# Gates of two heads on two halves of the rows, one chain for all other gates, and one copy for queries and keys of a pair, in a forgetting attention with a SwiGLU block

## The chip, the core and the metric

The kernel runs on one core of one Trainium2 chip. The metric is the device time of one execution in microseconds (us); several executions give a median. A hardware profile of one execution shows every instruction with its engine and its time. The engines are PE (matrix multiplication), PEld (its weight loads), DVE (VectorE), ACT (ScalarE), POOL (GpSimd) and SP (SyncE, which here only issues DMA transfers). POOL and ACT issue DMA transfers as well.

## The reference

q, k and v have 8 batches, 8 heads, 576 positions and 64 dimensions; f has 8 x 8 x 576. The attention adds a decay to the scores and feeds a gated block of 4608 tokens (8 x 576), 512 features and 1536 hidden features:

```python
scores = scale * np.matmul(q, k.transpose(0, 1, 3, 2))
log_f = np.log(np.clip(f, 0.0001, 1.0))
cum = np.cumsum(log_f, axis=-1)
decay = cum[:, :, :, None] - cum[:, :, None, :]
scores = np.where(causal, -1000000000.0, scores + decay)
attn = softmax(scores)            # with the maximum taken off first
x = matmul(attn, v), heads joined # 4608 x 512
g = x @ w_gate
out = (g * sigmoid(g) * (x @ w_val)) @ w_out
```

The values of `cum` are called gates here. A score needs `cum` of its query added and `cum` of its key taken off. In bfloat16 one number is too coarse for a key's gate, so it is kept as a sum of three (high, middle, low).

## The kernel before, in words

A small planner in the kernel (class `Plan`) decides the order of the instructions on each engine when the program is built. Each operation has an engine, an estimated duration, a key (lower goes first), a time `ready` before which it is not started, and what it waits for. On the chip each engine then runs its list strictly in that order and waits at semaphores. Constants such as `PACE0` (when batch 2's queries may be fetched) and `W_KEY` are inputs of this planner.

**Batch 0** is handled apart (`four`, `attention2`, `score2`). POOL loads q and k of eight heads by DMA, PE transposes them (L482), ACT and DVE copy them from PSUM into `QK` (L303 and L305 are the lines of the common copy helper: L303 on ACT, L305 on DVE or POOL). Head jj lies on rows 0 to 63 and head jj+4 on rows 64 to 127. A score group covers one of four parts of the key and query blocks for such a pair of heads (`BANKS`: 384, 512, 384 and 320 columns per head for the parts 0 to 3, so 1600 in all and 1216 in the parts 1 to 3). L641 multiplies queries and keys, 64 rows for each head. The gates are added by further matmuls into the same PSUM bank, over all 128 rows: `KG` holds the keys' gates of 32 heads in four row groups (a group of ones, high, middle, low), and the query side picks one head's rows. For the parts 1 to 3 this is L650, with a copy of the query side masked for that head (`choose`, L374). For the first part (the heads in `ONEHOT`, all of them) it is two matmuls without such a copy, L652 and L653.

**Gates.** `gates` loads f of batches 0 to 3 four times onto 128 rows, then clip (L324, DVE), ln (L327, ACT), a scan in two parts (L331, DVE) and the split into high, middle and low (L342 to L352). `dec_out` (L358) writes the rows for 32 heads to a DRAM buffer. The gates of batches 4 to 7 (32 heads on 32 rows, `lf1`) are loaded at the start and scanned and split later (`later`, L331, L362 to L370; `DEC1_AT = 36`), and four further `dec_out` write them.

**Batch 1** (`quad`): POOL loads q and k into natural order, PE transposes 128 columns at a time (`turn`, L498) with two pairs of heads one above the other in PSUM, and each half is copied to rows 0 to 63 of its pair's slot of `QK` (`straighten`, 16 copies of 64 rows). `rows` (L522) loads four gate rows for queries and keys from DRAM into rows 64 to 67 of that slot, so that one matmul of 68 rows (L623) gives score and decay together. Batches 2 to 7 get their transposed q and k through DRAM by DMA transposes on SP (`narrow`, `turned`) and their gate rows by `rows` as well.

**Then** ACT takes the exponential (L658), POOL masks the diagonal blocks (L667), PE multiplies with v (L681, 65 columns: 64 and one of ones for the sum), DVE takes the reciprocal and scales (L688, L693), and the result is transposed (L698 and a copy, or a DMA transpose on SP). The gated block is L826 (both first products), L830 (tanh on ACT), L834 and L837 (DVE), L841 (last product) and L845. The first 512 tokens go in two pieces of 256, woven into batch 1's attention. Idle PE is filled early by dummy matmuls (L930).

## Time and profile before

| what | us |
|---|---|
| median of 3 runs (lowest, highest) | 389.0 (388.3, 389.59) |
| the profiled execution's own time | 388.2 |
| span of its profile | 386.5 |
| first score of batch 0 (L641) | 10.43 |
| first score of batch 1 (L623) | 33.25 |
| first L841 | 67.75 |
| first score of batch 2 | 84.02 |
| last PE start | 382.85 |

The span runs from the first to the last instruction of the program in the profile. A busy share is an average over stages with different limits, so the stages are read one at a time: the table gives their borders. Where a line shows a group of instructions, the time from the start of one group to the start of the next says what the group costs in a stream; the duration of one matmul contains its way through the array and is longer. A wait is put down to what came last.

### The profile page before, as it was taken

How to read it: one execution, taken by the hardware profiler on the slowest of the kernel's cores; microseconds unless marked ns; L12 is line 12 of the kernel's file. 1: busy time of each engine (PE TensorE's matmuls, PEld its weight loads, DVE VectorE, ACT ScalarE, POOL GpSimd, SP SyncE). 2: the span in 40 equal slices, each digit the busy share in tenths (PEclk: the TensorE clock that was granted, in tenths of full speed). 3: DMA queues.
4: the chain of work that ended last, by engine and by line, in shares of the span. 5: the costliest groups of instructions: out<-in, count | busy, mean ns of one | idle time of the engine just before them, and what ended most of it. 6: DMA issues, size and time to landing. Idle time of an engine off the chain costs nothing.

```text
span 386.5 us, 8511 instructions
## 1 busy us (share of the span) xinstructions
PE 375.8 (97%) x3185; PEld 216.1 (56%) x3185; DVE 219.5 (57%) x460; ACT 213.8 (55%) x440; POOL 140.1 (36%) x368
## 2 busy tenths in 40 slices
PE   6997999999999999999999999999999999999996
PEld 4666789545556555555555555555564444444444
DVE  8957988257624773277515772477427725733750
ACT  5978884246756565755666457566673323323322
POOL 8794658005534624444355236522330000000000
PEclk9999999999999999999999999999999999999999
DMA  8999998769679994999699999995131011002003
GB/s 165 194 193 195 206 194 133 170 168 171 124 171 204 154 194 94 210 223 180 128 182 199 197 138 213 231 151 85 46 90 46 0 54 57 0 28 83 0 2 109
DMA packets 125065, 52.01 MB, mean 135 GB/s; under 512 B 111840, under 2 KB 119392, under 8 KB 124256
## 3 DMA queue, kind: packets, MB, share of 16 engines
q1 hardware_dynamic: 108640, 36.18, 46.9%
q0 software_dynamic: 16288, 15.14, 26.9%
q8 instruction: 25, 0.41, 0.4%
q10 hardware_dynamic: 96, 0.15, 0.1%
q14 instruction: 16, 0.13, 0.1%
HBM read 38.63 MB, written 17.11 MB: 144 GB/s over the span
## 4 chain that ended last, share of the span: by engine, by line
PE 94%; DVE 2%; ACT 2%; issue 1%; POOL 0%; DVEq 0%; POOLq 0%
PE ps L826 47%; PE ps L841 24%; PE ps L623 9%; PE ps L681 7%; PE ps L650 2%; ACT QK L303 1%; PE ps L641 1%; PE ps L930 1%; PE ps L698 1%; DVE QK L305 1%; PE ps L652 0%; DVE hh L837 0%; PE ps L482 0%; PE ps L498 0%; PE ps L653 0%
## 5 line engine op out<-in xcount | busy, mean ns | idle before, releaser
L826 PE MATMUL ps<-xT,wg 128*128 128x512 bf16 (+1 forms) x480 | 113.0, 357 | 1.1 <-DVE QK L305 1.0
L830 ACT ACTIVATE th<-ps 128x512 f32<-128x512 f32 (+1 forms) x120 | 66.5, 554 | 86.0 <-PE ps L826 83.6
L826 PE MATMUL ps<-xT,wv 128*128 128x512 bf16 (+1 forms) x480 | 113.0, 357 | 0.5 <-DMA wg<-in_moe_w_gate_dram 0.5
L834 DVE SCALAR_TENSOR_TENSOR th<-th,ps 128x512 f32<-128x512 f32 (+1 forms) x120 | 75.6, 630 | 64.9 <-ACT th L830 64.6
L658 ACT ACTIVATE PT<-ps 128x512 bf16<-128x512 f32 (+2 forms) x192 | 92.6, 508 | 27.6 <-PE ps L623 15.8
L841 PE MATMUL ps<-wo,hh 128*128 128x512 bf16 (+2 forms) x456 | 104.5, 367 | 0.0
L837 DVE TENSOR_TENSOR hh<-th,ps 128x512 bf16<-128x512 f32 (+1 forms) x120 | 76.0, 634 | 13.6 <-PE ps L826 1.8
L667 POOL TENSOR_SCALAR_AFFINE_SELECT PT<-PT 128x128 bf16<-128x128 bf16 (+1 forms) x192 | 52.9, 282 | 71.9 <-ACT PT L658 67.2
L826 PEld LDWEIGHTS <-wg 128*128 128x128 bf16 x480 | 45.5, 97 | 41.2 <-issue 1.4
L826 PEld LDWEIGHTS <-wv 128*128 128x128 bf16 x480 | 45.4, 97 | 37.5 <-issue 0.4
L623 PE MATMUL ps<-QK 68*128 68x256 bf16 x392 | 64.8, 261 | 0.0
L841 PEld LDWEIGHTS <-hh 128*128 128x128 bf16 x456 | 41.8, 97 | 37.1
L667 POOL TENSOR_SCALAR_AFFINE_SELECT PTa<-PTa 128x256 bf16<-128x256 bf16 x64 | 26.2, 412 | 76.1 <-ACT PTa L658 74.9
L688 DVE RECIPROCAL rc<-ps 128x5 f32<-128x5 f32 (+2 forms) x68 | 12.9, 190 | 65.5 <-PE ps L681 65.1
L681 PE MATMUL ps<-VB,PT 128*128 128x65 bf16 x768 | 44.2, 193 | 0.8 <-ACT QK L303 0.8
L681 PEld LDWEIGHTS <-PT 128*128 128x128 bf16 x768 | 37.0, 97 | 13.0 <-issue 1.0
L845 ACT ACTIVATE ot<-ps 128x512 f32<-128x512 f32 (+2 forms) x38 | 21.9, 575 | 39.9 <-PE ps L841 38.2
L623 PEld LDWEIGHTS <-QK 68*128 68x128 bf16 x392 | 31.1, 97 | 13.7
L658 ACT ACTIVATE PTa<-ps 128x384 bf16<-128x384 f32 x64 | 30.9, 488 | 10.3 <-PE ps L623 9.5
L693 DVE TENSOR_TENSOR xn<-ps,rc 128x320 bf16<-128x320 f32 (+2 forms) x72 | 32.3, 453 | 2.2
L681 PEld LDWEIGHTS <-PTa 128*128 128x128 bf16 x192 | 13.7, 98 | 11.3
L305 POOL CAST VB<-natv 128x512 bf16<-128x512 f32 (+1 forms) x32 | 19.0, 613 | 0.2 <-DMA natv<-in_v_dram 0.2
(69 smaller groups left out, 158.6 us busy)
## 6 DMA issues: line engine op xcount, KB each, us to landing
out_dram<-ot SPq DMA_DIRECT2D x35, 256.0 KB
natv<-in_v_dram SPq DMA_DIRECT2D x25, 256.0 KB
qk_d<-in_q_dram POOLq DMA_DIRECT2D x24, 144.0 KB, 3.6
qk_d<-in_k_dram POOLq DMA_DIRECT2D x24, 144.0 KB, 4.3
wg<-in_moe_w_gate_dram POOLq DMA_DIRECT2D x3, 512.0 KB, 11.1
wv<-in_moe_w_val_dram POOLq DMA_DIRECT2D x3, 512.0 KB, 12.4
wo<-in_moe_w_out_dram POOLq DMA_DIRECT2D x4, 384.0 KB, 11.9
xT<-in_q_dram POOLq DMA_DIRECT2D x4, 288.0 KB, 8.7
```

The lines of the kernel that those rows point to most:

```text
L305: E[e].tensor_copy(dst, src)
L623: nc.tensor.matmul(s[:, c : c + w], QK[:KR, hqk[p].i, 1, j * S + kt * P : j * S + (kt + 1) * P], QK[:KR, hqk[p].i, 0, j * S + q0 : j * S + ...
L658: nc.scalar.activation(place(h, i)[:, OFFS[i] : OFFS[i] + c], ps(bs)[:, :c], AF.Exp, scale=0.125)
L667: nc.gpsimd.affine_select(out=d, in_=d, pattern=pat, compare_op=ALU.is_ge, fill=0.0, base=0, channel_multiplier=-1,)
L681: nc.tensor.matmul(o[:, lo : lo + D + 1], pt[:, c : c + P], VB[hvb[b].i][:, kt, hb, : D + 1], start=first and n == 0, stop=last and n == l ...
L693: nc.vector.tensor_mul(XN[bx.i][:, qb : qb + nq, j], o, r)
L826: nc.tensor.matmul(ps(bf)[:, :n], w[:, ko, fc * P : (fc + 1) * P], xT[:, ko, t0 : t0 + n], start=(ko == 0), stop=(ko == KD - 1))
L830: nc.scalar.activation(TH[bt.i][:, :n], ps(bf)[:, :n], AF.Tanh, scale=0.5)
L834: nc.vector.scalar_tensor_tensor(out=t, in0=t, scalar=1.0, in1=ps(bf)[:, :n], op0=ALU.add, op1=ALU.mult)
L837: nc.vector.tensor_mul(HH[bh.i][:, lo : lo + n], TH[bt.i][:, :n], ps(bf)[:, :n])
L841: nc.tensor.matmul(ps(bf)[:m, c], HH[hs[fc].i][:, lo : lo + m], wo[:, fc, c], start=(fc == 0), stop=(fc == KF - 1))
L845: nc.scalar.activation(OT[bo.i][:m, c], ps(bf)[:m, c], AF.Copy, scale=0.5)
```

## The change

Four things are changed together.

1. **Batch 0's gates on halves of the rows.** f of batch 0 alone is loaded, eight times: rows 0 to 31 hold four copies of its 8 heads, rows 64 to 95 four more; the other rows are set to 1. In each half the 8-row groups of `KG` become ones, high, middle and low, by multiplying with constants per row (`ct`). A query side `QG[jj]` serves both heads of a pair, one on each half. So the gate matmuls have 64 rows for each head, as the score matmuls have. There are four masked copies for parts 1 to 3 instead of eight.
2. **All other gates in one chain.** `lf1` holds all 64 heads on 64 rows; the later chain makes all rows that go to DRAM, planned from 12 us on (`DEC1_AT`), and only its four `dec_out` are left. Its clip runs on POOL. The `rows` of batch 1 now wait for these.
3. **One copy for queries and keys of a pair.** `turn` puts q on rows 0 to 63 and k on rows 64 to 127 of PSUM for one pair; `straighten` copies 128 rows at once (8 copies in all). `lower`, a new DMA on SP, moves the keys to rows 0 to 63 of the pair's other half slot; `rows` of that pair follows it, since it writes over rows 64 to 67.
4. **Constants.** `PACE0` from 61 to 57; all five tiles of batch 1's v are cast by POOL's DMA (`V_CAST`), where two went through `natv`; smaller DMA durations in the planner, and the order of the transposes (`S1_KEY`, `U1`).

```diff
-    def ld_f(e, half, n):
-        E[e].dma_start(out=lf1 if half else lf[GR * n : GR * (n + 1)],
-                       in_=f.rearrange("b h s -> (b h) s")[GR * half : GR * (half + 1)])
+    def ld_f(e, n):
+        if n == 8:
+            E[e].dma_start(out=lf1, in_=f.rearrange("b h s -> (b h) s"))
+        else:
+            u, t = divmod(n, 4)
+            E[e].dma_start(out=lf[D * u + H * t : D * u + H * (t + 1)], in_=f[0])
...
+    def hi(e, c):
+        nc.vector.tensor_scalar_mul(KG[:, c], cum[:, c], -8.0)
+    def less(e, n, c):
+        nc.vector.scalar_tensor_tensor(out=r1[:, c], in0=KG[:, c], scalar=ct[:, 4 + n : 5 + n], in1=r1[:, c] if n else cum[:, c],
+                                       op0=ALU.mult, op1=ALU.add)
+    def mid(e, c):
+        nc.vector.tensor_scalar_mul(KG[:, c], r1[:, c], -8.0)
+    def low(e, c):
+        nc.vector.tensor_scalar(out=KG[:, c], in0=r1[:, c], scalar1=ct[:, 6:7], scalar2=ct[:, 3:4], op0=ALU.mult, op1=ALU.add)
...
+    def choose(e, jj, c):
+        s1, s2 = ct[:, 12 + jj : 13 + jj], ct[:, 8 + jj : 9 + jj]
         if e == "ACT":
+            nc.scalar.activation(QG[jj][:, c], cum[:, c], AF.Identity, scale=s1, bias=s2)
         else:
+            nc.vector.tensor_scalar(out=QG[jj][:, c], in0=cum[:, c], scalar1=s1, scalar2=s2, op0=ALU.mult, op1=ALU.add)
+    def dec_out(e, n):
+        nc.sync.dma_start(out=dec_dram[0, 0] if n == 0 else dec_dram[n, 1], in_=late[n])
...
-        out1 = [op(("SP", SPi), dec_out, 1, n, after=l, key=DEC1_KEY, dma=0.15, packet=50, tag="decout") for n in range(4)]
+        need = [l[:1], l[1:2], l[3:4], l[4:]]
+        out1 = [op(("SP", SPi), dec_out, n, after=need[n], key=-7, dma=0.3, packet=50, tag="decout") for n in range(4)]
...
-    def turn(e, b, g, x, n, bt):
+    def turn(e, g, u, n, bt):
         t0, nt = PH[n]
         t = ps(bt).bitcast(BF16)
         for i in range(nt):
-            for u in range(2):
-                nc.tensor.transpose(t[D * u : D * (u + 1), i * P : (i + 1) * P],
-                                    QN[b][2 * g + x][:, u, (t0 + i) * D : (t0 + i + 1) * D], ident)
+            for x in range(2):
+                nc.tensor.transpose(t[D * x : D * (x + 1), i * P : (i + 1) * P],
+                                    QN[1][2 * g + x][:, u, (t0 + i) * D : (t0 + i + 1) * D], ident)
...
+    def straighten(e, p, n, bt):
         t0, nt = PH[n]
+        dst = QK[:, hqk[p].i, 0, : 2 * S].rearrange("p (j c t) -> p j c t", j=2, t=QT)[:, :, :, t0 : t0 + nt]
+        copy(e, dst, ps(bt).bitcast(BF16)[:, : nt * P].rearrange("p (t j c) -> p j c t", t=nt, j=2))
+    def lower(e, p):
+        nc.sync.dma_start(out=QK[:D, hqk[p].i, 1, : 2 * S], in_=QK[D:, hqk[p].i, 0, : 2 * S])
...
+            done.append(op(("SP", SPi), lower, p, after=done, use=[hqk[p]], key=key, dma=0.5, packet=93, tag=("lower", p)))
+            r = op(("SP", SPi), rows, p, after=done + out1 + o_out1, use=[hqk[p]], key=key, dma=0.25, packet=60, tag=("rows", p))
...
         for n, (kt, q0, w, c) in enumerate(segs):
             for u in range(2):
-                s, h, end = ps(bs[u]), jj + 4 * u, n == len(segs) - 1
-                m = min(P, S - kt * P)
-                keys = KG[:, kt * P : kt * P + m]
+                r, m, end = slice(D * u, D * (u + 1)), min(P, S - kt * P), n == len(segs) - 1
+                o, keys = ps(bs[u])[:m, c : c + w], KG[r, kt * P : kt * P + m]
                 if i or jj not in ONEHOT:
-                    row = G1[h][:, q0 - HALF : q0 - HALF + w] if i else G0[h][:, q0 : q0 + w]
-                    nc.tensor.matmul(s[:m, c : c + w], keys, row, start=False, stop=end)
+                    nc.tensor.matmul(o, keys, QG[jj][r, q0 : q0 + w], start=False, stop=end)
                 else:
-                    nc.tensor.matmul(s[:m, c : c + w], keys, three[:, h : h + 1].to_broadcast([P, w]), start=False, stop=False)
-                    nc.tensor.matmul(s[:m, c : c + w], ident[:, GR + h : GR + h + 1].to_broadcast([P, m]),
-                                     QG[:, q0 : q0 + w], start=False, stop=end)
+                    mine = D * u + 3 * H + FB * u + jj
+                    nc.tensor.matmul(o, keys, one[r, jj : jj + 1].to_broadcast([D, w]), start=False, stop=False)
+                    nc.tensor.matmul(o, ident[r, mine : mine + 1].to_broadcast([D, m]), QS[r, q0 : q0 + w], start=False, stop=end)
...
-CLIP1 = ('DVE', 0.43)
+CLIP1 = ('POOL', 2.1)
-V_CAST = {0: 5, 1: 3}
+V_CAST = {0: 5, 1: 5}
-DEC1_KEY = 9000
-DEC1_AT = 36
+DEC1_KEY = 1000
+DEC1_AT = 12
-PACE0 = 61.0
+PACE0 = 57.0
```

In the changed kernel the lines of the first steps move: L641 becomes L644, L650 becomes L651, L652 and L653 become L654 and L655, L623 becomes L626, L303 and L305 become L302 and L304, L331 becomes L334, L681 becomes L682 and L826 becomes L827. `lower` is L512 and `rows` L529.

167 lines of the change are left out of this document (70 added, 97 removed).

## Prediction

> **What bounds the kernel now.** I read the page first, then busy times by stretch, the waits, the chain from 28 to 38 us, PE's timeline, and last the DMA queues, because the change puts new transfers ahead of batch 1.
>
> ```profile
> span 386.5 us, 8511 instructions
> PE 375.8 (97%) x3185; PEld 216.1 (56%) x3185; DVE 219.5 (57%) x460; ACT 213.8 (55%) x440; POOL 140.1 (36%) x368
> ...
> PE 94%; DVE 2%; ACT 2%; issue 1%; POOL 0%; DVEq 0%; POOLq 0%
> ```
>
> PE carries 94% of the chain, so a microsecond taken from PE's work or waits is a microsecond of the end, unless another wait takes its place. The stretches say where waits are (columns: stretch, length, busy PE, PEld, DVE, ACT, POOL, granted clock, DMA share, GB/s):
>
> ```profile
> 17.00:27.00 10.00, 10.00 (x142) 6.55 (x140) 5.18 (x24) 8.38 (x20) 9.98 (x29) 1.00 1.24 204
> 27.00:33.25 6.25, 5.40 (x112) 4.21 (x111) 4.91 (x11) 4.71 (x9) 2.89 (x9) 1.00 1.70 175
> 33.25:46.00 12.75, 10.48 (x117) 8.57 (x115) 10.54 (x25) 11.85 (x27) 8.29 (x19) 1.00 1.24 206
> 46.00:67.75 21.75, 21.75 (x285) 19.41 (x283) 18.76 (x52) 14.43 (x37) 15.06 (x37) 1.00 0.98 167
> ```
>
> From 46 to 290 us PE never rests. Everything this change can give or take lies before 46 us. In 17 to 27 PE is full and DVE half idle; from 27 to 46 PE waits. For whom, the chain shows (start, us):
>
> ```profile
> 29.87 0.83 DVE QK L305
> 30.72 0.78 ACT QK L303
> ...
> 32.42 0.83 DVE QK L305
> 33.27 0.78 ACT QK L303
> ...
> 36.49 0.74 ACT QK L303
> ...
> 37.26 0.73 DVE QK L305
> ```
>
> These are batch 1's 16 straightening copies. PE's timeline shows two scores side by side and two gates one after the other:
>
> ```profile
> 17.91 0.31 PE L641 MATMUL ps<-QK 64*128 64x320 bf16 x2
> 18.15 0.45 PE L650 MATMUL ps<-xT 128*128 128x320 bf16 x2
> ```
>
> The two 64-row L641 take 0.24 to the next start, the two 128-row L650 0.28. Single starts say more: the two L641 start 3 ns apart, and 0.095 us of their 0.24 is a pause where the shape changes from 64 to 128 rows.
>
> Last, a small transfer by SP, and the DMA queues in 18.6 to 21.85, then in 21.85 to 24.4 us (packets, MB, share):
>
> ```profile
> 17.85 2.76 SPq L522 DMA_DIRECT2D QK<-dec_d  x4
> ```
> ```profile
> q0 software_dynamic: 635, 0.65, 120.8%
> q8 instruction: 1, 0.02, 1.9%
> ```
> ```profile
> q0 software_dynamic: 441, 0.49, 112.2%
> q1 hardware_dynamic: 44, 0.06, 8.0%
> ```
>
> The first of the four `rows` was issued by 18.62, yet SP's queue q1 moves nothing until 21.87: 3.25 us. The gate rows of L358, issued at 11.22 and 45.58, first move at 14.87 and 48.63 (3.65, 3.05). POOL's queue is full all that time. Before it is, an `f` load issued at 1.21 moves at 1.85 (0.64).
>
> **The change part by part.**
>
> *Gate matmuls on half the rows.* Summed from start to next start, L641, L652, L653 and L650 take 4.42 + 1.36 + 1.80 + 5.06 = 12.6 us. After it, L651's pairs run as L641's do: 1216 columns per pair of heads, four pairs, at 2.4 columns/ns, 2.0 us instead of 4.1. The one-hot pairs are issued two to a head, so only neighbours overlap: 0.43 instead of 0.65 us, four times, -0.9. The 0.095 pauses fall from 2.25 to about 1.5 per score group, since L644 and L651 now share a shape: -1.1 over 16 groups. Together -4.0 (bounds -3, if the one-hot rows don't overlap at all, to -4.6, if three pauses in four go).
>
> *Start.* The lf memsets of 576 columns cost 0.6 each (128x288 took 0.30), +0.55. Eight small operations build `ct` and `one` where three took 0.54: at the same 0.15 each, +0.55. The clip starts at 5.5 instead of 4.53. clip1 leaves DVE (-0.9), the chain from `hi` to `low` gains one step (+0.46) on 128 rows instead of 64 (same columns, same time). ACT issues four `f` loads, not two (+0.9); the table load of 1.28 still ends before ln needs it. The first scores need the copy of k behind scan part 1: 11.2 instead of 10.43, +0.8 (0 to +1.5). clip1 on POOL has no row: between the 0.6 of a POOL cast (L305) and 2.7, three times the 0.91 it takes on DVE. POOL starts it near 6.5, after four q/k loads and two V loads, and ACT's ln1 wants it at 9.2, so both ends are hidden. Behind it on POOL wait three V loads and the first two weights, which stand in a full DMA queue later anyway.
>
> *Straightening, 16 copies to 8.* PE's pauses by these copies: 0.47 and 0.70 before 33.25, then 0.50, 0.56, 1.12, 0.31, 0.24 and 0.09 from start to start (the 0.95 that the page shows for the longest leaves out a matmul's tail): 4.0 us go. The copies have the same 640 and 512 columns over 128 rows, 0.75 each. What is late next: batch 0's exps on ACT and the transfers below. I leave 0.4 of new waits after the first batch-1 score (0 to 1).
>
> *All other gates in one chain.* L331, L364, L366, L368, L370 (1.34, 0.56, 0.74, 0.50, 0.74) stand at 41.8 to 48.9 now. They go to about 15 to 20 us, where DVE is half idle, on 64 rows instead of 32. Costed at nothing; if the cover is gone, batch 0's norms move by up to 3.9. The four dec_out and the `edge` (3.0 now) leave SP by about 23.5.
>
> *Batch 1's V, all by POOL.* Two more issues of 0.85 on POOL, two natv loads and two casts (0.60) fewer, and as many bytes from HBM: nothing: behind them stand the second third of the weights, issued at 24.3 and 25.6 now, landed 11 to 12 us later, and first used at 47.1.
>
> *Lower and rows.* Now a pair's four `rows` are fetched at 17.85, long before use. After it, a pair's last copy releases `lower` (64 packets of 2304 bytes) on SP; `rows` waits for `lower` to land; the scores wait for `rows`. When is the first pair straightened? ACT reaches batch 0's exps at 13.9 (ln to 6.8, three copies of 0.6, `up`, ln1, 1.28 of table, two picks and three copies behind them). Eight PTa exps at 0.39 and L367 end at 17.6. Then, at 0.50, 0.39 and 0.34 for the three PT forms, two pairs, one x copy, th and the third pair's start: 24.0. Its copy of pair 4 ends at 24.7; the other half is on DVE behind a silu and four norm steps, 26.0. With 0.3 of small waits, 26.3. Then `lower`: 0.1 + 0.45 issue + 3.3 to the first packet + 0.8 to land (the 32 packets of a dec_out took about 0.6) = 4.65; `rows`: 0.05 + 0.7 + 3.3 + 0.5 = 4.55. First batch-1 score at 35.5; it is at 33.25 now. The nearest rows for 3.3 are the four at 3.05 to 3.7, all under the same full queue; the other end is the idle queue's 0.64.
> From 11.2 to that score PE has, in its new order: scores and gates 8.6, 36 transposes 0.6, 110 L681 at 0.03, 14 flips at 0.056, 72 batch-1 transposes at 0.03, 12 FFN matmuls at 0.109, and some 20 pauses: 18.9 of 24.3 us. So 5.4 us are waits: about 1.3 for ACT, the rest for the two transfers.
> Pair 5's `rows` sit behind two more waits on SP and land some 5.4 us later, as PE gets there (5.4 us of scores and FFN lie between). Batch 2's five natv loads and pair 8's transposes wait behind pair 7's `rows` on SP; they are issued at 49.2 and 60.7 now, SP is through by about 39.
>
> *PACE0 57.* Batch 2's narrow loads on POOL and transposes on SP come 4 us earlier. Now rows for pair 8 are issued at 75.6 and used at 84.0, over 5 us of slack: nothing, 0 to +1.
>
> **Sum:** -4.0 (gates) + 0.8 (start) - 4.0 (pauses by copies) + 0.4 (new small waits) + 5.4 (waits before batch 1) = -1.4. The profiled execution took 388.2 (span 386.5 and 1.7 around it): 386.8. It lies 0.8 under the median of 389.0, so I predict 387.6.
>
> **Rivals.**
>
> *The transfers take as little as on an idle queue.* With 0.64 to the first packet the two take 4.0 us, `rows` lands at 30.3, and ACT's exps set the start: batch 0's last ends near 30.3, with 1.1 of waits 31.4. Then -5.5: 383.5. For it: q1 carries little, and only POOL's queue is full. Against: four instances of over 3 us, none shorter while POOL's queue was full.
> [...]
>
> *The pause halves PE's clock (slower).* PE's first 17 dummies, 256 columns each, take 3.68 us, 0.216 each; the same 256 columns take 0.11 at 12.45. So PE runs at half rate after rest, and the change makes a pause of some 4 us at 31.4 to 35.5 where the longest now is 1.1. If 3.7 to 7.4 us after it (one to two times that first stretch) run at half rate, 1.8 to 3.7 are lost: -1.4 becomes +0.4 to +2.3, 389.4 to 391.3. It decides from 1.4 us of loss, 2.8 us at half rate. Against: the granted clock is 1.00 throughout, and some L681 may fall into the pause.
> [...]
>
> *ACT is later than I count.* If batch 0's exps or DVE's norms reach pair 4 at 27.8 instead of 26.3, all of the chain moves: +1.5, no change, 389. ACT is 84% busy in 17 to 27 already.
>
> **How the numbers follow.** Two transfers limit, as summed: 0.50. Fast transfers 0.20, half clock 0.18, later ACT 0.12. A measurement tells some 0.3%, 1.2 us, from no change. Of the 0.50, 0.34 is faster, 0.14 the same, 0.02 slower; the fast transfers are all faster; half clock is 0.15 slower and 0.03 the same; later ACT 0.01, 0.06, 0.05: faster 0.55, same 0.23, slower 0.22. The likeliest case alone spans 386.3 to 389.0 (pair 4 straightened at 25.5 to 27, 3.05 to 3.65 to each first packet). Range 383.4 to 390.7: the fast transfers' end, and most of the half clock's.
>
> **What would show it.** L651 x2 starting 3 ns apart and next starts 0.14 later; eight L302/L304 copies to QK of about 0.75; L334 on 64 rows before 20 us; `lower` and `rows` each over 4 us on the way and the first L626 near 35.5 behind a wait for DMA; no idle PE from 46 on. Wrong if that L626 comes by 32 (fast transfers) or after 37, or if matmuls of 256 columns after the pause take 0.21.

## The result and the profile after

| | before | after |
|---|---|---|
| median (lowest, highest), us | 389.0 (388.3, 389.72) | 395.21 (394.64, 396.76) |
| ratio to before, 95% interval | | 1.0157 (1.0131 to 1.0182) |
| own time and span of the profiled execution | 388.2, 386.5 | 394.64, 392.9 |
| first score of batch 0 | 10.43 | 12.39 |
| start of the first and end of the last mask of batch 0's first parts | 12.02, 18.92 | 15.79, 21.49 |
| first score of batch 1 | 33.25 | 42.19 |
| first last product (L841, now L842) | 67.75 | 74.74 |
| last PE start | 382.85 | 389.11 |

The change costs 6.2 us, where 1.4 were forecast to be gained. The measurement lies 4.5 us above the range. The new lines are L644 (score, L641 before), L651 (its gates, L650), L654 and L655 (the one-hot gates), L626 (batch 1's score, L623), L302 and L304 (the copies on ACT and on DVE or POOL), L334 (scan), L327 (clip), L330 (ln), L363 (`dec_out`), L512 (`lower`), L529 (`rows`), L668 (mask), L682 (the product with v) and L827 (the first products of the block). The page of after, its totals and its chain by engine:

```profile
span 392.9 us, 8466 instructions
...
PE 373.3 (95%) x3144; PEld 215.1 (55%) x3186; DVE 217.1 (55%) x453; ACT 211.1 (54%) x436; POOL 142.8 (36%) x369
...
PE 89%; DMA 5%; POOL 3%; issue 1%; DVE 1%; ACT 0%; SPq 0%; DVEq 0%
```

The chain through PE falls from 94% to 89%: DMA, which before's chain does not list, and POOL, 0% there, carry 8% now. (PE shows 3144 matmuls and 3186 weight loads, where before shows 3185 of each: records are missing, so its busy time here is too low, and small gaps late in the span are not waits. From the first L826 or L827 of the second block of tokens, at 78.84 before and 85.10 after, to the last PE start it is 304.0 us in both. All the loss lies ahead of that.) Now the stretches that the prediction read, before 46 us and one earlier (columns: stretch, length, busy PE, PEld, DVE, ACT, POOL, granted clock, DMA share, GB/s), first of before, where the stretch from the first score on was not shown:

```profile
10.43:17.00 6.57, 6.54 (x138) 4.92 (x138) 6.34 (x20) 5.74 (x13) 4.54 (x8) 1.00 1.95 184
```

and of after:

```profile
10.43:17.00 6.57, 3.87 (x110) 3.00 (x103) 6.43 (x13) 6.54 (x13) 6.57 (x10) 1.00 1.92 177
17.00:27.00 10.00, 8.59 (x113) 5.11 (x108) 7.33 (x23) 7.70 (x20) 10.00 (x19) 0.83 1.22 213
27.00:33.25 6.25, 6.25 (x118) 4.19 (x117) 4.57 (x13) 4.96 (x11) 6.25 (x19) 1.00 1.94 176
33.25:46.00 12.75, 7.29 (x108) 5.71 (x107) 4.86 (x15) 4.85 (x12) 5.12 (x12) 0.87 1.22 228
...
21.45:24.86 3.41, 3.41 (x30) 1.66 (x28) 2.37 (x10) 1.30 (x4) 3.41 (x5) 0.50 1.20 222
...
41.95:45.35 3.40, 3.16 (x24) 2.44 (x25) 1.41 (x5) 1.58 (x3) 0.69 (x2) 0.50 1.22 231
```

Three things stand in these rows. From 10.43 to 17 PE was full and now rests 2.7 of 6.57 us, while DVE, ACT and POOL are full. In two stretches of 3.4 us the granted clock is 0.50. And from 33.25 to 46 PE rests 5.5 us. What it rests for is in PE's waits of after from 10 to 46 us (engine, operand, line, what it waited for: us, times, longest):

```profile
PE ps L626 <- DMA QK<-dec_d: 5.5, 1, 5.5
PE ps L486 <- DVE QK L304: 1.5, 1, 1.5
PE ps L682 <- POOL PTa L668: 1.4, 3, 0.7
PE ps L931 <- ACT QK L302: 1.1, 1, 1.1
```

and for the first of them in the chain of after (start, us, what):

```profile
29.25 0.36 DVE xn L694
29.61 0.64 DVE QK L304
...
30.30 6.41 DMA QK<-QK
36.71 0.02 issue
36.73 5.32 DMA QK<-dec_d
42.05 0.14 issue
42.19 0.48 PE ps L626 x2
```

Batch 1's straightening copies, which stood in before's chain one after another, are down to one. Behind it come `lower`, which the change put in, and `rows`, which now waits for it: 11.7 us of chain. By the DMA queues, `lower` of two pairs moves its first packets at 34.31, 4.0 us after the issue, and `rows` its first at 40.78, 4.05 after. PE's pauses of before (2.27 us idle from 33 to 46, 1.4 of them for the copies) are gone as forecast, and a single wait of 5.5 stands in their place.

Why the masks are late is in POOL's timeline of after (start, us, engine, line, operation, names, count, idle before):

```profile
8.21 2.14 POOL L327 TENSOR_SCALAR QK<-QK 64x576 f32<-64x576 f32 x1 [1.49 <-DMA QK<-in_f_dram]
10.41 2.54 POOL L535 DMA_DIRECT2D VB<-in_v_dram  x3
12.89 0.82 POOL L823 DMA_DIRECT2D wg<-in_moe_w_gate_dram  x1
13.64 0.81 POOL L823 DMA_DIRECT2D wv<-in_moe_w_val_dram  x1
...
15.79 0.87 POOL L668 TENSOR_SCALAR_AFFINE_SELECT PTa<-PTa 128x256 bf16<-128x256 bf16 x2
...
18.03 3.46 POOL L668 TENSOR_SCALAR_AFFINE_SELECT PTa<-PTa 128x256 bf16<-128x256 bf16 x6
```

The clip waits 1.5 us for its f and takes 2.14, and all that POOL has to issue follows it. On ACT, the ln of `lf1`, which waits 1.35 us for this clip, stands ahead of the table load and of all else (ACT's timeline of after):

```profile
10.38 0.68 ACT L330 ACTIVATE QK<-QK 64x576 f32<-64x576 f32 x1 [1.35 <-POOL QK L327]
11.08 1.28 ACT L456 ACT_TABLE_LOAD   x1
...
15.17 3.21 ACT L659 ACTIVATE PTa<-ps 128x384 bf16<-128x384 f32 x8
```

So the first exponential starts at 15.17 (11.46 before) and the first mask at 15.79. Two more loads from 16.60 to 18.03 part the masks, and the last of the first eight ends at 21.49, when ACT has been through with their exponentials since 18.38. PE's 1.4 us of waits for masks are here.

A ledger of PE up to 70 us, in us, worked out from PE's starts:

| | before | after | difference |
|---|---|---|---|
| gate matmuls of batch 0 (at full clock) | 12.64 | 8.2 | -4.4 |
| useful work done before 10.43 (idle and dummies there 9.18, 8.48) | | | -0.7 |
| idle 10.43 to 33 | 0.87 | 4.11 | +3.2 |
| dummies in it | 0 | 1.23 | +1.2 |
| idle 33 to 46 | 2.27 | 5.46 | +3.2 |
| half clock, two stretches of 3.41, half of each lost (estimate) | 0 | 3.4 | +3.4 |
| sum | | | +5.9 |

The last PE start moved by 6.26. The half clock's row is an upper estimate: 0.5 us of dummies and 0.2 us of rest lie in the two stretches, and it takes PE's own work as the limit in all the rest. So the matmul saving came as forecast, and up to 11 us of waits, dummies and slow clock came with it.

### The profile page after: what moved, and what is told of

It reads as the page before. It is cut to its first block, busy times and chain, and to the rows that moved or that the text cites. A ratio compares the mean times of both kernels' runs of the same rounds, so it can differ in the third digit from the quotient of the medians.

```text
span 392.9 us, 8466 instructions
## 1 busy us (share of the span) xinstructions
PE 373.3 (95%) x3144; PEld 215.1 (55%) x3186; DVE 217.1 (55%) x453; ACT 211.1 (54%) x436; POOL 142.8 (36%) x369
## 4 chain that ended last, share of the span: by engine, by line
PE 89%; DMA 5%; POOL 3%; issue 1%; DVE 1%; ACT 0%; SPq 0%; DVEq 0%
PE ps L827 46%; PE ps L842 24%; PE ps L626 10%; PE ps L682 7%; DMA QK<-QK 2%; DMA QK<-in_f_dram 1%; DMA QK<-dec_d 1%; POOL PTa L668 1%; POOL xT L478 1%; PE ps L699 1%; POOL VB L535 1%; POOL QK L327 1%; PE ps L644 0%; PE ps L651 0%; DMA xT<-in_f_dram 0%
## 5 line engine op out<-in xcount | busy, mean ns | idle before, releaser
L827 PE MATMUL ps<-xT,wg 128*128 128x512 bf16 (+1 forms) x473 | 112.5, 358 | 0.4
L827 PE MATMUL ps<-xT,wv 128*128 128x512 bf16 (+1 forms) x461 | 110.6, 358 | 1.0 <-DVE hh L838 0.2
L842 PE MATMUL ps<-wo,hh 128*128 128x512 bf16 (+2 forms) x440 | 102.3, 367 | 0.8
L668 POOL TENSOR_SCALAR_AFFINE_SELECT PT<-PT 128x128 bf16<-128x128 bf16 (+1 forms) x192 | 51.9, 276 | 69.1 <-ACT PT L659 64.5
L626 PE MATMUL ps<-QK 68*128 68x256 bf16 x392 | 65.9, 262 | 5.5 <-DMA QK<-dec_d 5.5
L827 PEld LDWEIGHTS <-wg 128*128 128x128 bf16 x480 | 46.1, 98 | 40.1
L827 PEld LDWEIGHTS <-wv 128*128 128x128 bf16 x480 | 44.9, 98 | 37.5 <-issue 0.4
L842 PEld LDWEIGHTS <-hh 128*128 128x128 bf16 x456 | 42.3, 97 | 37.4
L668 POOL TENSOR_SCALAR_AFFINE_SELECT PTa<-PTa 128x256 bf16<-128x256 bf16 x64 | 27.1, 428 | 81.7 <-ACT PTa L659 80.9
L682 PE MATMUL ps<-VB,PT 128*128 128x65 bf16 x768 | 44.9, 194 | 0.1
L682 PEld LDWEIGHTS <-PT 128*128 128x128 bf16 x768 | 37.3, 98 | 13.1 <-issue 0.3
L846 ACT ACTIVATE ot<-ps 128x512 f32<-128x512 f32 (+2 forms) x38 | 21.9, 575 | 36.2 <-PE ps L842 32.5
L626 PEld LDWEIGHTS <-QK 68*128 68x128 bf16 x392 | 30.9, 98 | 18.7 <-issue 5.6
L682 PEld LDWEIGHTS <-PTa 128*128 128x128 bf16 x192 | 13.5, 98 | 13.6 <-POOL PTa L668 1.3
L304 POOL CAST VB<-natv 128x512 bf16<-128x512 f32 (+1 forms) x30 | 18.0, 614 | 0.0
```

The costliest lines, as they stand in the source:

```text
L304: E[e].tensor_copy(dst, src)
L626: nc.tensor.matmul(s[:, c : c + w], QK[:KR, hqk[p].i, 1, j * S + kt * P : j * S + (kt + 1) * P], QK[:KR, hqk[p].i, 0, j * S + q0 : j * S + ...
L668: nc.gpsimd.affine_select(out=d, in_=d, pattern=pat, compare_op=ALU.is_ge, fill=0.0, base=0, channel_multiplier=-1,)
L682: nc.tensor.matmul(o[:, lo : lo + D + 1], pt[:, c : c + P], VB[hvb[b].i][:, kt, hb, : D + 1], start=first and n == 0, stop=last and n == l ...
L827: nc.tensor.matmul(ps(bf)[:, :n], w[:, ko, fc * P : (fc + 1) * P], xT[:, ko, t0 : t0 + n], start=(ko == 0), stop=(ko == KD - 1))
L842: nc.tensor.matmul(ps(bf)[:m, c], HH[hs[fc].i][:, lo : lo + m], wo[:, fc, c], start=(fc == 0), stop=(fc == KF - 1))
```

## The experiments

Each kernel was timed beside the kernel before on the same chip; ratios are to it, with a 95% interval. "Half clock" means a stretch in which the granted clock is 0.50.

### The parts, one at a time on the kernel before

**The gate matmuls on half the rows and nothing else.** Every matmul of batch 0's gates reads 64 of the 128 rows; the order of all engines stays. It leaves out half of each gate sum, so batch 0's decay is incomplete.

```diff
-                keys = KG[:, kt * P : kt * P + m]
+                r, keys = slice(D * u, D * (u + 1)), KG[D * u : D * (u + 1), kt * P : kt * P + m]
...
-                    row = G1[h][:, q0 - HALF : q0 - HALF + w] if i else G0[h][:, q0 : q0 + w]
+                    row = G1[h][r, q0 - HALF : q0 - HALF + w] if i else G0[h][r, q0 : q0 + w]
```

> The kernel before, with PE's gate matmuls alone altered: each takes half of the rows of its operands (rows 0 to 63 for the one head of a pair, 64 to 127 for the other), in the same order; all other engines do exactly what they do before. It leaves out half of each gate sum, so the decay of batch 0 is incomplete. It measures what the first part of the change is worth by itself. Theory B (PE is the bound, as the prediction has it): the gate groups fall from 12.6 to 8.2 us and the time falls by 3 to 4.5 us, to 385 to 386. Theory H (the helpers bound): from 10 to 33 us POOL is 100% and ACT 84% busy in the kernel before, so PE waits for exponentials, masks and copies instead, and less than half of it is seen: 387.5 to 389. If the waits trip the clock to 0.50 it is 389 to 390.

Measured: 387.42 us, ratio 0.9974 (0.9957 to 0.999), a gain of 1.0 us (0.4 to 1.7). PE's work in batch 0 falls by 4.2 us. The stretches of this kernel show where the other 3.2 stayed:

```profile
10.43:17.00 6.57, 5.26 (x143) 4.01 (x143) 6.34 (x20) 5.97 (x15) 5.17 (x9) 1.00 1.95 184
17.00:27.00 10.00, 9.27 (x160) 6.15 (x160) 6.06 (x26) 8.65 (x21) 9.98 (x28) 1.00 1.24 203
```

PE is no longer full: it rests 1.3 and 0.7 us where before it rested 0.03 and 0, with waits such as these (PE's waits of the same kernel):

```profile
PE ps L482 <- DVE QK L305: 0.8, 1, 0.8
PE ps L681 <- POOL PT L667: 0.6, 1, 0.6
...
PE ps L681 <- POOL PTa L667: 0.4, 1, 0.4
```

DVE's 6.34 of 6.57 and POOL's 9.98 of 10 hardly move. These helpers stood right behind PE; a microsecond taken from PE here, with the old order kept, is worth a quarter of one (0.1 to 0.4 by the interval). What an order planned for the shorter matmuls would give, this run does not show.

**Two constants alone**: `V_CAST = {0: 5, 1: 5}` and `PACE0 = 57.0`.

> The kernel before with two constants of the change alone: all five of batch 1's V loads by POOL, and the pace of batch 2's queries at 57. The prediction costs both at nothing. Theory S (the loss is made of the slow first masks, the two new transfers and the half clock; constants carry none of it): 388.5 to 389.5 us, ratio 0.998 to 1.002. Rival C (POOL, busy 9.98 of 10 us from 17 to 27, hands its two more issues of 0.85 us on to batch 1's straightening or to the weights): +0.8 to +1.7 us, ratio 1.002 to 1.0045, with the first score of batch 1 (L622 behind L305's or L303's copies) later than 33.25 us by as much.

Measured: 388.43 us, ratio 0.9991 (0.9981 to 1.0001). The constants carry none of the loss, although the first score of batch 1 moved from 33.25 to 34.52.

**The late gate chain alone, run early**, on its 32 rows:

```diff
-DEC1_KEY = 9000
-DEC1_AT = 36
+DEC1_KEY = 1000
+DEC1_AT = 12
```

> The kernel before with the late gate chain of batches 1 to 3 (the scan of L331 and the five operations behind it, on 32 rows) run early, from 12 us on, instead of at 41.8 to 48.9. The prediction costs it at nothing, and at up to 3.9 us of later norms of batch 0 if its cover is gone. Theory S (DVE is busy only 5.18 of 10 us from 17 to 27, so the chain has room): 388.3 to 389.6 us, ratio 0.998 to 1.002, the chain done by 24 us. Rival C (the chain stands in front of batch 0's silu, norms and masks on DVE, and PE waits): +1.5 to +3.9 us, ratio 1.004 to 1.010, with the first score of batch 1 later than 33.25 us.

Measured: 393.79 us, ratio 1.0122 (1.0093 to 1.015), 4.7 us slower. This was forecast at nothing. The chain runs from 17.96 to 24.35, and two stretches of before and then of this kernel show what it meets:

```profile
17.00:21.00 4.00, 4.00 (x52) 2.50 (x50) 2.99 (x14) 3.57 (x9) 4.00 (x9) 1.00 1.24 206
21.00:25.00 4.00, 4.00 (x66) 2.80 (x65) 1.16 (x5) 3.39 (x9) 4.00 (x14) 1.00 1.20 211
```
```profile
17.00:21.00 4.00, 3.95 (x54) 2.46 (x51) 3.93 (x12) 3.55 (x10) 4.00 (x8) 1.00 1.24 208
21.00:25.00 4.00, 3.05 (x38) 1.79 (x36) 3.25 (x9) 2.30 (x7) 4.00 (x9) 1.00 1.22 213
```

DVE was half idle from 17 to 27 only on average: 2.99 of 4 us until 21, then 1.16. The scan of 1.54 us comes in the busy part, ahead of reciprocals of batch 0 (L688, from 19.43 on), and the chain's other four stand among the norms until 24.35. PE goes from 4.00 to 3.05 in the second stretch. The profiled execution is the fastest of the four (392.01 us, a span of 390.3 where before's is 386.5), with a clock of 1.00 from the first score on; the other three had a mean granted clock of 0.989 to 0.990 and took 393.52 to 394.23, so part of the 4.7 goes with slow stretches that this profile doesn't show. The waits that it names are small (the longest 1.3 for L305, 1.0 for L303, 0.9 for masks in two). Idle PE from 10.43 to 46 accounts for 1.6 of the 3.8 us of span (0.87 + 2.27 became 1.74 + 2.95). The planner also put batch 0's last scores at 39.98, where they were at 28.55; how much of the rest is that new order and how much the full DVE stays open.

**One copy, `lower` and `rows` behind it, alone** (the new `turn`, `straighten`, `lower` and `quad`; the gates stay as before):

> The kernel before with the third part of the change alone: one copy for queries and keys of a pair (8 copies in place of 16), the keys lowered by a transfer, the gate rows behind it; gates, constants and all else as before. Theory T (two transfers in a row): lower and rows take 9 to 12 us from the last copy of pair 4, PE waits 3 to 6 us ahead of batch 1 and then runs 3.4 us at a granted clock of 0.50; the pauses by copies (4.0 us) go: 390 to 393. Rival: pair 4 is straightened by 24 to 25 us, as batch 0 is not late here, the 9.2 us of the prediction end at 33.5 to 34.5, the wait is under 2 us and the 4.0 us of pauses show: 386 to 388.

Measured: 393.11 us, ratio 1.0115 (1.009 to 1.0139), 4.5 us slower. PE's waits and SP's timeline of this kernel (L507 is `lower`, L524 `rows`):

```profile
PE ps L622 <- DMA QK<-dec_d: 4.1, 1, 4.1
```
```profile
29.33 1.96 SPq L507 DMA_DIRECT2D QK<-QK  x2
34.77 0.78 SPq L524 DMA_DIRECT2D QK<-dec_d  x1
```

From the issue of `lower` to the first score at 40.22 it is 10.9 us. The gate rows were on the way to DRAM early here, so the two transfers in a row, and not late gates, make this wait. Half clock from 39.6 to 46.4 follows. Of the 5.3 us by which the last PE start is later, 3.4 lie ahead of the second block of tokens and 1.8 behind its start, with waits of 0.8 for a mask and 0.4 for a norm among them; this part is left open.

**The halves alone.** Batch 0's gates on half rows as in the change, with the spare rows of `KG` kept for batch 1's gates (eight loads of 16 rows of f), so that the late chain stays at 36 us, `rows` of batch 1 stay early, and parts 3 and 4 of the change are left out; clip of `lf1` on DVE. Some of its edits, against the changed kernel:

```diff
-            u, t = divmod(n, 4)
-            E[e].dma_start(out=lf[D * u + H * t : D * u + H * (t + 1)], in_=f[0])
+            E[e].dma_start(out=lf[2 * H * n : 2 * H * (n + 1)], in_=f[:2].rearrange("b h s -> (b h) s"))
...
-CLIP1 = ('POOL', 2.1)
+CLIP1 = ('DVE', 0.9)
...
-DEC1_KEY = 1000
-DEC1_AT = 12
+DEC1_KEY = 9000
+DEC1_AT = 36
```

> The gates on halves without the other parts, as in the version with spare rows tried before (393.2), but f of batches 0 and 1 comes by eight transfers of 16 rows in place of four with repeated rows, which landed as late as 9.8 us, and f of the other gates is loaded first. Theory S (only f's late landing held that version): f lands by 6 to 6.5, the first score comes at 10.5 to 11.5, the stretch of 13.6 us at half clock goes, and the time is under that of the kernel before by 1 to 3 us: 386 to 388. Theory H (the helpers bound): DVE, ACT and POOL are full from 9 to 20 us, as gates on 128 rows, copies and loads all lie there; PE has waits of 2 to 4 us and at least one stretch of 3.4 us at half clock: 390 to 392.

Measured: 388.58 us, ratio 0.9993 (0.9978 to 1.0008). The first score is at 13.77, 3.3 us later than before, and this stretch of it is at half clock:

```profile
9.85:16.65 6.80, 6.33 (x139) 4.90 (x138) 6.45 (x14) 5.58 (x11) 3.71 (x6) 0.50 1.89 188
```

and still the median is level with before, so the gates pay for so late a start. They do not clearly pay for the slow stretch as well: this execution took 389.55 us, and the five of the ten with a mean granted clock of 0.999 or 1.000 took 387.93 to 389.42.

Alone, the pieces give -0.3 (halves, with another start than the change's), +4.7 (early chain), +4.5 (transfers), -0.3 (constants): 8.6 us, more than the 6.2 of all together. So they overlap: with the transfers taken out of the change, for one, `rows` still waits for the late gates (next part). How the 6.2 split among them is not shown.

### The change with one piece taken back

**Without the one copy** (two copies of 64 rows again, no `lower`; `rows` waits for the early gate chain only):

```diff
-            done.append(op(("SP", SPi), lower, p, after=done, use=[hqk[p]], key=key, dma=0.5, packet=93, tag=("lower", p)))
-            r = op(("SP", SPi), rows, p, after=done + out1 + o_out1, use=[hqk[p]], key=key, dma=0.25, packet=60, tag=("rows", p))
+            r = op(("SP", SPi), rows, p, after=[o_qkz] + out1 + o_out1, use=[hqk[p]], key=key, dma=0.25, packet=60, tag=("rows", p))
```

> The changed kernel without its third part's copy and transfer: each pair of batch 1 is straightened by separate copies of queries and keys to rows 0 to 63 (16 copies), there is no transfer that lowers the keys, and the gate rows are loaded as soon as the gates are in DRAM. Theory T (transfers): the two transfers in a row take 6.4 and 5.3 us, PE waits 5.5 us for them and then runs 3 us at half clock. Without them pair 4 is ready at about 31, the wait at 36.7 to 42.2 goes and with it the half clock: 7.1 us, of which the pauses by eight more copies take back 0 to 4: 388 to 392, taken as 390. Rival: batch 0's lateness sets the time, PE waits for ACT's exponentials and copies instead, and the gain stays under 2 us: 393 or more.

Measured: 392.05 us, ratio 1.0072 (1.0057 to 1.0087). The first score of batch 1 is at 36.38, still behind a wait of 2.2 us for `rows`, because the four `dec_out` leave from 20.60 to 25.69 and `rows` at 30.70. So part 3 costs 3.3 us here, and 2.8 remain. Half clock remains too, from 13.75 to 20.65 and from 37.65 to 41.1.

**The same with `CLIP1` on DVE** (`('DVE', 0.9)`):

> The changed kernel with both alterations of two earlier runs at once: the clip of the other gates on DVE, and separate copies of queries and keys without the transfer of the keys. What is left of the change is the gates on halves, the one chain for all other gates, and the constants. If the two causes add up (1.6 us and 3.2 us gained against the changed kernel), it takes 390.5. Theory G (gates of batch 1 late): rows of batch 1 now wait for the late chain's writes to DRAM; with separate copies they are issued at 30.7 and land at 36, and PE waits 2.2 us for them, so the two causes do not add up in full and the time stays above the kernel before, at 390 to 392. Rival: with both gone nothing else is in the way, the 4 us of the gate matmuls show, and the time is 385 to 387.

Measured: 393.18 us, ratio 1.0104 (1.0084 to 1.0124), slower than with the clip on POOL (the intervals just touch), although the first score of batch 0 came at 9.59 and that of batch 1 at 33.04. The masks ended at 21.99, where they ended at 20.25 with the clip on POOL; whether that is the reason stays open.

**`CLIP1` on DVE, all else as in the change:**

> The changed kernel with one constant altered: the clip of the other gates runs on DVE again (its list on DVE, ACT and POOL is planned anew). Theory P (POOL's list): in the changed kernel POOL waits with the clip until f lands at 8.2 us and clips until 10.34; all issues behind it come late, two of batch 1's query loads fall between the masks of batch 0, the masks end at 21.1 us although their exponentials end at 18.4, and PE waits 1.4 us for them and then runs 3 us at a granted clock of 0.50. Without the clip the masks follow the exponentials, the stretch at half clock before 25 us goes, pair 4 is straightened by about 27 instead of 30.2, and the time falls by about 3.5 us, to 391.7. Rival F (the loads of f): the other gates' f lands at 8.1 us whichever engine clips it, ln, the table load and the exponentials keep their place, and DVE has 0.9 us more: the time stays at 395 or rises by up to 1.

Measured: 393.63 us, ratio 1.0114 (1.0082 to 1.0147), 1.6 us better than the change by the medians, though the intervals overlap. The first score came at 9.65 and yet the first exponential at 15.01 and the first mask at 16.97: POOL, without the clip, waited 1.29 and 1.73 us for earlier transfers of its own to land, ahead of batch 1's q and k, and the masks ended at 21.83. So taking the clip off POOL did not bring the masks forward, against the expectation; the loads ahead of them hold them too. Half clock lasted from 15.05 to 21.9 and from 42.35 to 45.8.

**The planner's DMA durations as before, on top of that:**

> The changed kernel with the clip of the other gates on DVE and with the planner's durations of POOL's transfers as before (1.8, 3.1 and 2.5 in place of 1.65, 2.6 and 1.95), which only alters the planned order. Theory O (order on POOL): with the clip on DVE alone POOL still had all four query and key loads of batch 1 ahead of the first mask, waited 3.0 us for earlier transfers before them, and the masks of batch 0's first part ended at 21.8 as in the changed kernel, though they ended at 18.9 before. With the old durations one of the four comes behind the first mask; if POOL's order ahead of the masks is what holds batch 0, the masks end 0.5 to 1 us earlier and the time falls to 392.5 to 393. Rival: the order by one load does not matter, 393.6 as with the clip alone.

Measured: 396.78 us, ratio 1.0199 (1.0181 to 1.0216). The masks ended at 20.80, but the first score of batch 1 came at 42.59 after a wait of 5.9, with half clock from 39.2 to 46.05, and the time from the first last product to the last PE start rose from 314.4 to 317.5. The new order brought the masks forward and lost more behind them.

**Batch 0's f in two loads** (each reads its 8 heads four times):

```diff
-            u, t = divmod(n, 4)
-            E[e].dma_start(out=lf[D * u + H * t : D * u + H * (t + 1)], in_=f[0])
+            E[e].dma_start(out=lf[D * n : D * n + D // 2], in_=f[0].unsqueeze(0).to_broadcast([4, H, S]))
```

> The changed kernel with f of batch 0 loaded by two transfers (each reads the 8 rows four times over) in place of eight of 8 rows; the clip of the other gates stays on POOL. Rival F (the loads of f): in the changed kernel the last of the eight lands near 6.0 us, DVE's first clip starts at 6.30, the load of the other gates is issued at 2.49 and lands at 8.1, and the first score comes at 12.39 instead of the 11.2 predicted. With two loads both land 1.5 to 2 us earlier, and all of batch 0 with them: first score at 11 to 11.5, pair 4 straightened by 28.5, time 393 to 394. Theory P alone: POOL's clip starts a little earlier too, so part of the same gain, but the masks stay behind their exponentials by 2 us or more and PE still has a stretch at half clock before 25 us.

Measured: 395.75 us, ratio 1.0161 (1.0131 to 1.0191), no gain. The first exponential moved from 15.2 to 12.06, the first mask only to 15.03, since POOL issues loads from 9.2 to 15.03. Masks ended at 22.06. PE ran at half rate until 14.6 in the profiled execution (a matmul of 256 columns took 0.21 us to the next start, 0.11 from then on; the granted clock is given as 1.00 there), so this run does not show what an earlier f is worth at full rate.

**The identity matrix ahead of POOL's q and k loads** (`key=-50` instead of -18), so that those loads start later beside f:

> The changed kernel with one key altered: POOL writes the identity ahead of its first query and key load (0.6 us later loads; the plan behind it shifts by itself). Theory L: in the changed kernel the last of f's eight small loads lands at 6.0 us and the other gates' f at 8.1, since POOL's loads of q and k fill the DMA engines from 3.0 us on; loads that move first land by 4 to 5 and by 7, DVE's first clip starts by 5.9 (its own list ends then), POOL's clip by 7, the first masks follow by 13 to 14 in place of 15.8, and the time falls by 1 to 2.5 us, to 393 to 394. Rival P: POOL's list of issues (clip, five loads of v, two weights, quads) is as long as before and holds the masks; the time stays at 395 within 0.7.

Measured: 394.44 us, ratio 1.0155 (1.0106 to 1.0204), no gain that the scatter of its four executions (393.04 to 398.75) would show. Batch 0's clip began at 5.75 and POOL's at 7.45, each under 1 us earlier.

**The wait filled with dummies** (48 matmuls of 256 columns ahead of batch 1's first score):

```diff
         s, c = ps(bs), 0
+        for _ in range(48 if h == H and i == 0 else 0):
+            nc.tensor.matmul(s[:, :HALF], ident, ident.unsqueeze(1).to_broadcast([P, 2, P]), start=True, stop=True)
```

> The changed kernel with 48 dummy matmuls of 256 columns (some 5.1 us at full rate) put on PE right ahead of the first score of batch 1, where PE waits 5.5 us for a transfer; they write a PSUM bank that the score then overwrites. Theory C (clock): after the wait PE runs from 42.2 to about 45.2 us at a granted clock of 0.50, which costs about 1.6 us. With the dummies the granted clock there is 1.00, the first score of batch 1 stays at about 42.2, and the time falls by 1.4 to 1.8 us, to 393.6. Rival: the matmuls after the wait are held by ACT and the masks anyway, so the half rate costs nothing: 395 within 0.5, with the clock at 1.00. If the dummies end late, the first score comes later than 42.2 and the time rises.

Measured: 394.06 us, ratio 1.0122 (1.0106 to 1.0139), 1.15 us under the change by the medians, with intervals that just overlap. Two stretches of this kernel:

```profile
21.35:24.75 3.40, 3.30 (x33) 1.75 (x30) 2.82 (x12) 1.38 (x5) 3.40 (x7) 0.50 1.16 199
41.95:45.35 3.40, 3.40 (x45) 2.90 (x43) 1.90 (x7) 2.22 (x5) 0.96 (x4) 1.00 1.20 237
```

The second slow stretch is gone, the first is untouched. So the wait before batch 1 does halve the clock after it, for one stretch of 3.4 us: 0.50 with the wait, 1.00 with it filled. Half of that stretch would be 1.7 us; 1.15 came back.

**POOL's queue kept quiet during the transfers** (the second and third thirds of the weights and `wo` not before 50 us, so that the total says nothing):

```diff
-W_AT = [2.0, 2.0, 2.0]
-WO_AT = 20.0
+W_AT = [2.0, 50.0, 54.0]
+WO_AT = 58.0
```

> The changed kernel with the second and third thirds of the first weights and all of the last weights loaded by POOL only from a planned 50 us on, in place of 28 to 40 us; nothing else is altered, and its total time is of no use, since the block waits for its weights. It asks what the two transfers of batch 1 cost when POOL's queue is empty. Theory Q (POOL's full queue): in the changed kernel lower is issued at 30.30 and moves its first packet at 34.31 (4.0 us), rows is issued at 36.73 and moves at 40.78 (4.05). With POOL's queue empty from about 33 us on, rows moves its first packet within 1.5 us of its issue and has landed within 2.5 us, in place of 5.3, and lower is quicker by up to 2 us. Rival L (a fixed cost of such a transfer in the middle of a kernel): both still take 3 to 4 us to the first packet.

SP's timeline of this kernel:

```profile
30.12 1.56 SPq L512 DMA_DIRECT2D QK<-QK  x2
33.66 0.76 SPq L529 DMA_DIRECT2D QK<-dec_d  x1
```

`lower` moves its first packet about 1.1 us after its issue instead of 4.0, as POOL's queue runs empty, and `rows` 1.5 after its issue instead of 4.05, with nothing else on the way. Batch 1 starts at 36.93 with no wait for a DMA (total 400.91 in the one execution, from the late weights). So some 2.5 of the 4 us go with POOL's full queue and are not the transfer's own. Whether the weights that fill it can be moved for less than they cost at 50 us was not tried.

### Towards a version that beats before

> A version that keeps the gates on halves and drops the rest: batch 1 is straightened by separate copies; the rows of the gate tile that the changed kernel fills with 1 hold batch 1's gates (one more group: 8 times the sum, high, middle, low), so that its gate rows go to DRAM from batch 0's own chain as before; the chain for batches 2 to 7 runs late as before, its clip on DVE; f is loaded by four transfers of 32 rows; the constants and the planner's durations are as before. Theory S (the halves are worth what was worked out, and only the other three parts cost): no wait for a transfer ahead of batch 1, no stretch at half clock, first score of batch 1 at 30 to 33, and the time is 3 to 4 us under the kernel before: 385 to 386.5. Rival: the start is later by 1 to 2 us through f's loads and the longer chain, pauses by the 16 copies fill with the time that the gates save, and the time is that of the kernel before, 388 to 390.

The halves alone with f in four loads, each of which writes one batch's 8 heads four times: 393.16 us, 1.0102 (1.0083 to 1.0121). The clip started at 9.85, the first score came at 15.25, and half clock lasted from 9.7 to 23.35, four stretches. This led to the eight loads of the version above, where the clip could start at 8.88.

> The version with the gates on halves alone (eight loads of 16 rows, batch 1's gates on the spare rows, late chain as before, separate copies), with the start mended: POOL writes the identity (0.6 us) ahead of its first query and key load, so that f's loads move before POOL's queue fills, and the other gates' f comes after f of batch 0. In the version before this one f landed at 8.7 us, the first score came at 13.8 in place of 10.4, PE had waits of 2.1 us and 6.8 us at half clock at the start, and yet the time equalled that of the kernel before. Theory L (f lands late because its later loads share the DMA engines with POOL's): f lands by 6, the first score comes at 11 to 12, at most one stretch of 3.4 us at half clock is left, and the time is 385 to 387, under the kernel before. Rival H (the helpers bound): the start moves up by 2 us and more, but DVE and ACT hold the copies and the gates, PE waits as long as before, and the time stays within 1 us of the kernel before.

With the identity first and `lf1` loaded after f: 389.9 us, 1.0027 (1.0013 to 1.0041). DVE waited 1.05 us for `lf1`; half clock from 12.85 to 16.25.

> The same version without the longer dummies: only the clip of the other gates behind batch 0's first part. If the clock matters at the start, a stretch of 3.4 us at 0.50 stays and this run is 1 to 2 us slower than the one with the longer dummies; if it does not, because copies and gates hold PE there anyway, the two are equal within 0.5 us.

The same with the clip of `lf1` behind the first part of batch 0's gates: 389.8 us, 1.0036 (1.002 to 1.0052), first score at 12.36 and no half clock after the start in the profiled execution.

> The version with the gates on halves alone and the identity first (389.9), with two more alterations at the start: the clip of the other gates comes on DVE behind batch 0's first part (it waited 1.05 us for its f in the middle of that chain, and took 0.83), and the dummy matmuls that the planner puts into PE's idle time have 512 columns from the 27th on and go to the bank that has been free longest (256 columns and the one freed last before, where they waited for a copy). Theory S (the start alone holds the halves back): the first score comes at 11.5 to 12.5 in place of 14.2, no stretch at half clock is left, and the time is 385 to 387, under the kernel before. Rival H (the helpers bound): the start moves up, but DVE and ACT hold the copies and exponentials, and the time stays within 1 us of the kernel before, 388 to 390.

And with longer dummies at the start: 390.17 us, 1.0036 (1.0021 to 1.0051), no half clock there either, so the two do not show what the dummies are worth. An even clock did not bring the halves below before. None of the versions that compute the whole result is shown to be faster than the kernel before.

## Why the prediction was wrong, by its steps

**Gate matmuls, -4.0: the size right, its worth wrong.** PE's timeline of after:

```profile
25.02 0.31 PE L644 MATMUL ps<-QK 64*128 64x320 bf16 x2
25.16 0.30 PE L651 MATMUL ps<-xT 64*128 64x320 bf16 x2
```

The pair's next start is 0.14 us on, as forecast, and the groups fell by 4.4 us. But the sum took "a microsecond taken from PE's work is a microsecond of the end" from a chain that was 94% PE. The gate matmuls alone brought 1.0 of 4.2. The condition that the same sentence named, another wait taking its place, was met. The prediction's own stretches had shown POOL busy 9.98 of 10 us from 17 to 27; the stretch from 10.43 to 17, with DVE busy 6.34 of 6.57, it did not show.

**Start, +0.8, and 0.4 of new waits: mis-sized.** The first score came at 12.39, not 11.2, and idle PE and dummies up to 33 us grew by 4.4 us, 0.7 of them paid back by work done earlier. "Both ends hidden" for the clip on POOL failed at both. Its start needed `lf1`, which landed at 8.12, where I had POOL free near 6.5 and never asked for the data. Its end, at 10.34 where ACT wanted it at 9.2, put off ACT's ln, table load and exponentials, and on POOL what is issued there and the masks behind it: first mask 15.79 instead of 12.02. I had said that these loads "stand in a full DMA queue later anyway"; but their issues stand in POOL's own stream, ahead of the masks, and took it from 10.41 to 14.37. As price for the clip, 0.6 to 2.7 held it (2.14). What this step cost is not isolated: with the clip on DVE the exponentials and masks were no earlier.

**The gate chain, costed at nothing: the step with the largest single miss.** Alone it costs 4.7 us, more than the 3.9 that the prediction gave as its price "if the cover is gone". The cover was read as 5.18 of 10 us from 17 to 27. Read in 4 us steps, DVE was 75% busy where the scan starts, and every norm of batch 0 goes through that engine. In after the scan starts at 16.96 and the chain ends at 24.0. That is the price on the kernel before, with its own new order; after's chain of waits does not pass through these five operations, so their share of the 6.2 is not isolated.

**Pauses by 16 copies, -4.0: right that they go, too much put down to the copies.** From 27 to 33.25 PE is full, and in the chain one copy is left. But three of the pauses in the sum (0.56, 0.31 and 0.24) were not for copies. PE's waits of before:

```profile
PE ps L826 <- DMA wg<-in_moe_w_gate_dram: 0.5, 1, 0.5
...
PE ps L698 <- DVE xn L693: 0.2, 1, 0.2
PE ps L826 <- DVE th L834: 0.2, 1, 0.2
```

With 16 copies put back into the change, PE waited 0.95 us for them from 26 us on. So no run shows the 4.0 us as gained by the one copy.

**Lower and rows, a wait of 5.4: right by number, wrong in both its ends.** The wait was 5.46, but it ended at 42.19 instead of 35.5. Pair 4 was straightened at 30.24, not 26.3: by the chain, the masks held PE until 21.14, PE then worked on without a wait until 28.5, 3.4 us of it at half clock, and DVE's norms and the copy at 29.61 followed. `lower` took 6.41 for 4.65 and `rows` 5.46 for 4.55: the first packets came after 4.0 us, not the 3.3 taken from rows at 3.05 to 3.65, and the data of `lower`, two pairs of which moved together, took 2.4 us where 0.8 was counted. PE in its turn ran out of work only at 36.7. That the wait came out as forecast is luck: the two errors cancelled in the wait, not in the time. The rival with fast transfers was wrong here, and nearer once the queue is quiet: 1.1 and 1.5 us, between this case and the 0.64 of the rival.

**The half clock: the rival happened, and twice.** It was priced at 1.8 to 3.7 us; the ledger's upper estimate is 3.4 for two stretches, and filling the wait ahead of the second gave back 1.15. The filled wait shows the second stretch as made by the wait for `rows`. The first, from 21.45, follows no such wait. From 18.04 to 21.45 PE is busy 0.59 of the time, between pauses of 0.71, 0.50 and 0.20 for masks. The prediction looked for one pause of some 4 us and left out that several short ones may do the same; that these pauses made the first stretch is likely, but no run fills them. Nor is the price of a slow stretch fixed: after's five executions took 394.64 and 395.27 us at a mean granted clock of 0.991, and 394.69, 395.21 and 396.76 at 0.978 to 0.983.

**ACT later than counted** also came about, in a larger size: pair 4 at 30.24 where the rival had 27.8. The prediction gave each rival its price as if it came alone, and bounded the range by the half clock's. Late masks, slower transfers and the slow clock are not independent here, since late masks and late transfers make the pauses ahead of the slow stretches; they came together, with the early chain: 6.2 us, where the highest single case gave 2.3.

## What to carry to other kernels

When one engine holds 94% of the chain, look in steps of a few microseconds at how full the engines behind it are before counting its savings, and before hiding new work on them: an average over 10 us had room for the chain, the place where it landed had little. A DMA put into a dependent chain is to be priced with its latency under the traffic of that moment (here 4.0 and 4.05 us to the first packet beside a full queue, 1.1 and 1.5 beside a quiet one), and two in a row with twice that. Rivals that share a cause belong into one case with the sum of their prices.

## What the runs showed of the hardware

**The slow stretches were 3.4 us long or a multiple.** This holds for every stretch with a granted clock of 0.50 seen up to 55 us (3.4 in after, 6.8 in the transfers alone, 13.6 with f in four loads). The first dummies are not among them: they run at half rate too (0.216 us each in before), at a granted clock that the profile gives as 1.00, and with f in two loads this lasted until 14.6. In these kernels the 3.4 us ahead of a slow stretch had PE busy 0.00 to 0.67 of the time, dummies counted, and where it was 0.56 (the change without the one copy, 10.39 to 13.80) or 0.59 (after), its pauses were of 0.2 to 1.5 us. Yet after's 35.11 to 38.52, which begins three times 3.41 us behind the end of its first slow stretch, had PE busy 1.61 of 3.41 us (0.47) with no slow stretch behind it; the next 3.41 us, without a matmul, had one. So the busy share alone does not tell where a slow stretch follows; what does stays open.

**How early f lands does not follow from its bytes or its number of loads.** Four loads of 72 KB let the clip start at 4.53 in before and at 9.85 with f written four times over; eight of 36 KB at 8.88 in the halves alone and at 6.47 with the identity first and `lf1` behind f; eight of 18 KB at 6.30 (after) and two of 72 KB at 5.13. In each of the two pairs with equal loads the earlier clip had its last load of f of batch 0 issued earlier (1.27 against 2.06 us, 2.20 against 3.00), all beside POOL's loads of q and k from 1.3 to 1.5 us on. Whether that order is the cause, the runs do not separate.
